# Loading w_in in natural row order, and laying the heads of Y onto the partitions of their features by copies and transfers

## The chip, the cores and the metric

The kernel runs on one core of a Trainium2 chip. A core has five engines with a queue of instructions each: TensorE (PE in the profile; its weight loads are PEld) multiplies matrices from SBUF into PSUM, VectorE (DVE), ScalarE (ACT) and GpSimd (POOL) work elementwise, and SyncE (SP) issues the DMA transfers of this kernel. Every queue is worked off in order. Waits between engines are semaphores, which the tile framework sets from what each instruction reads and writes. The metric is the device time of one execution in microseconds (us), lower is better.

## The reference

Two parts, joined by a transposition. The first is a delta-rule recurrence over 768 positions, for 4 batch elements and 8 heads of dimension 48:

```python
k_n = k / (np.linalg.norm(k, axis=-1, keepdims=True) + 1e-06)
for t in range(S):
    kt, vt, bt = (k_n[:, :, t], v[:, :, t], beta[:, :, t, None])
    y[:, :, t] = np.einsum('bhd,bhde->bhe', q[:, :, t], state)
    v_old = np.einsum('bhde,bhd->bhe', state, kt)
    state = state + bt[:, :, :, None] * np.einsum('bhd,bhe->bhde', kt, vt - v_old)
```

The second takes y as x, 3072 tokens of 384 features (feature = 48 x head + index in the head), through a feed-forward with 2048 hidden units:

```python
x = np.ascontiguousarray(attn_out.transpose(0, 2, 1, 3)).reshape(B * S, H * D)
h = x @ w_in
g = h * (1.0 / (1.0 + np.exp(-h)))
return (g @ w_out).astype(np.float32)
```

q, k, v and beta are float32. w_in (384 x 2048) and w_out (2048 x 384) come as float64: 8 bytes an element, 6.3 MB each.

## The kernel before, in words

**Chunks.** The 768 positions are cut into 6 chunks of 128 (the partitions). A chunk is treated for the 4 batch elements together, in a chain of stages:

- *prepare*: `turn` transposes k and q on TensorE (L376), `score` multiplies them (L399) and masks the products into `ap` on ScalarE and VectorE (L409, L415). `block_out` and `block_in` bring the 32 x 32 diagonal blocks through DRAM into a tile `g` with one block a partition (L443, L451). `block_out` also clears the tile `x` on GpSimd (L438). `scale` and `size` multiply k and v on GpSimd (L352, L360).
- *invert*: the 128 unit triangular blocks (4 batch elements x 8 heads x 4), one a partition, are inverted on VectorE, in 30 steps of two instructions (L477, L481). The results go to DRAM (L492) and come back in two orders into `xe` and `xis` (L502). `invert` is a generator; in chunk 0 the loop that draws it counts the steps as n.
- *solve*: `merge` (L551) joins pairs of blocks, then a pipeline over the batch elements x, with step k from 0 to 6: `inner` and `across` (L583, L591) solve for the new values, `add` (L574) subtracts between the halves on VectorE, `keep` (L601) copies the result z to SBUF on ScalarE, `old` (L614) and `new` (L642, L648) make Y in the PSUM bank `pys[x]`, and `update` (L625, L632) brings the state forward. The norms of the next chunk's keys are drawn in the same loop: `squares` at n = 5 (L306, L309) and `norms` at n = 6 (15 small VectorE instructions from L320 to L338).
- *feed_forward*: `hidden` (L719) multiplies Y, transposed with features on partitions as `xT`, by w_in, two batch elements (256 tokens) at a time. Silu goes through ScalarE (L729). Chunk 0 ends in `project` (L742), the later ones in `combine` (L813), which needs 7 products of half size instead of 8, by adding parts of w_out and of the hidden values (`sum_w`, `sum_g`, L795).

**Order.** The order on every engine is that of the program: `pin` ties each instruction to the one before it on its engine, `in_line` does so for the DMA transfers of SyncE, all in one queue. The feed-forward of one chunk is a generator, `pieces`, and the loops at the end of the program draw from it between the steps of the next chunk's prepare, invert and solve. In the beginning, where there is no feed-forward yet, `busy` issues dummy products (L276): 20 of them follow the 18th step of chunk 0's inversion.

**Weights.** float64 is narrowed on the chip. `narrow` takes three steps over ScalarE (L165, L170), VectorE (L167, L173, L177) and GpSimd (L181) for each of 8 pieces of w_in (256 columns) and 8 of w_out. The raw pieces lie in tiles that are free at that time: the later homes of w_out (`room`), tiles of tag `gT`, sums for `combine` (`sums_of_g`, `sums_of_w`). `fetch_w_in` (L215) and `fetch_w_out` (L245) issue the loads. `queue` holds the pieces to narrow, `fill(n)` issues n steps, `more` fetches a piece of w_out once another is narrowed.

**Where Y's features lie.** A PSUM bank holds Y of one batch element as 4 column blocks of 128 tokens, for the head pairs 0 to 3: even heads on partitions 0 to 47, odd heads on 64 to 111. TensorE wants 3 x 128 features on partitions. So before the change the kernel fills the gaps 48 to 63 and 112 to 127 with thirds of the last pair's heads, and the rows of w_in are loaded in that order:

```python
(at, lambda a, e=e, n=n: (2 * a + e) * D if n == D else (6 + e) * D + a * (W - D), n)
```

That makes 4 transfers a piece: 48 and 16 partitions in each half. In chunks 1 to 5 `new` copies the last pair (L662) and the 48 rows of each half (L665), and 6 transfers carry the thirds (L669). Chunk 0, where the state is zero, gets the thirds from TensorE: `keep` copies a third of the last pair beside each head (L605) and a product more is added for it (L648).

Of the kernel before, what the change touches and what calls it, by code (L numbers as in the profile page):

```python
# [21 lines left out]
def kernel(  # L22
# [120 lines left out]
    for load_one in (load_k, load_q):  # L143
# [4 lines left out]


    ROWS = [  # L150
        (at, lambda a, e=e, n=n: (2 * a + e) * D if n == D else (6 + e) * D + a * (W - D), n)
        for e in range(2)
        for at, n in ((W * e, D), (W * e + D, W - D))
    ]
# [44 lines left out]
    def fetch_w_in(i):  # L199
        if i < 4:  # L200
            raw = room(1 - i // 2, i % 2)
        elif i < NWI - 1:
            raw = mlp.tile([P, SIZE], U32, name="raw", tag="gT", bufs=3)[:]
        else:
            raw = spare
        raw = raw.rearrange("p (a f) -> p a f", a=NKT)
        for at, row, rows in ROWS:
            step = row(1) - row(0)
            src = moe_w_in[row(0) : row(0) + rows, i * WF : (i + 1) * WF].bitcast(U32)
            pitch = src.ap[0][0]  # L210
            src = bass.AP(
                tensor=src.tensor, offset=src.offset,
                ap=[[pitch, rows], [pitch * step, NKT], [1, 2 * WF]],
            )
            in_line(nc.sync.dma_start(out=raw[at : at + rows], in_=src))  # L215
        raws[i] = raw.rearrange("p a (f j) -> p a f j", j=2)
# [7 lines left out]
    sums_of_w = [const.tile([P, NFF // 2, HM], FP32, name=f"sums_of_w{i}") for i in range(3)]  # L224

    def narrow_w_in(i):
        return narrow(w_in[:, :, i * WF : (i + 1) * WF], raws.pop(i))
# [3 lines left out]
    def fetch_w_out(i):  # L231
        if i in (0, 1, 5):
            raw = room(1, min(i, 1))
        elif i in (4, 7):
            raw = sums_of_w[2 if i == 4 else 0][:].rearrange("p f m -> p (f m)").bitcast(U32)
        elif i == 6:
            raw = spare
        else:
            k = int(i == 3)
            if k not in places:  # L240
                places[k] = work.tile([P, SIZE], U32, name="raw_out", tag="ap", bufs=4)
            raw = places[k][:]
        raw = raw.rearrange("p (a f) -> p a f", a=2)
        src = moe_w_out.rearrange("(a p) f -> p a f", p=P)[:, 2 * i : 2 * i + 2, :].bitcast(U32)
        in_line(nc.sync.dma_start(out=raw, in_=src))  # L245
        raws[i] = raw.rearrange("p a (f j) -> p a f j", j=2)

    def narrow_w_out(i):
        at = 2 * i % HFF
        return narrow(w_outs[2 * i // HFF][:, at : at + 2, :], raws.pop(i))  # L250
# [45 lines left out]
    def squares(c):  # L296

        sums[c] = small.tile([P, BH], FP32, name="ss", bufs=1)[:]
        for b in range(B):
            if c == 1:  # L300
                sq = packed(zbufs[b])
            else:
                if b % HB == 0:
                    two = work.tile([P, HB, H, D], FP32, name="sq", tag="xg"[b // HB], bufs=1)
                sq = two[:, b % HB]
            pin(nc.scalar.activation(  # L306
                out=sq, in_=packed(kbufs[(c * B + b) % NK]), func=ACTF.Square
            ))
            pin(nc.vector.tensor_reduce(  # L309
                out=sums[c][:, b * H : (b + 1) * H], in_=sq, axis=AX.X, op=ALU.add  # L310
            ))
# [141 lines left out]
    def invert(c):  # L453
# [41 lines left out]
        if c == 0:  # L495
            xe = sums_of_w[1][:].rearrange("p f m -> p (f m)")[:, 0 : BH * T]
            xes[c] = xe.rearrange("p (n t) -> p n t", n=BH)
        else:
            xes[c] = work.tile([P, BH, T], FP32, name="xe", tag="x", bufs=1)[:]
# [13 lines left out]
    xTs, xes = {}, {}  # L513

    def solve(c, us):
# [6 lines left out]
        pzs, pys, third = {}, {}, {}  # L522
# [5 lines left out]

        if c == 0:
            pin(nc.gpsimd.memset(sums_of_w[0][:], 0.0))  # L530
            thirds = sums_of_w[0][:].rearrange("p f m -> p (f m)").rearrange(
                "p (x k e w) -> p x k e w", x=B, k=NKT, e=2
            )
            third = {x: thirds[:, x] for x in range(B)}
# [65 lines left out]
        def keep(x, rows):  # L600
            pin(nc.scalar.copy(  # L601
                z_of(x)[rows, :, :, 0:D], pzs[x][rows].rearrange("p (a e) d -> p a e d", e=2)
            ))
            if c == 0:
                pin(nc.scalar.copy(  # L605
                    third[x][rows, :, :, D:W],
                    pzs[x][rows, H - 2 : H, :].rearrange("p e (a n) -> p a e n", a=NKT),
                ))
# [28 lines left out]
        def new(x):  # L637
            z, ap = z_of(x), us[x]["ap"]
            for p in range(NP if c > 0 else NKT):
                for e in range(2):  # L640
# [3 lines left out]
                        start=(c == 0), stop=(c > 0), skip_group_check=True,  # L644
                    ))
                for e in range(2 if c == 0 else 0):
                    at = slice(W * e, W * (e + 1)), slice(C * p, C * (p + 1))
                    pin(nc.tensor.matmul(  # L648
                        pys[x][at], lhsT=third[x][:, p, e, :], rhs=ap[:, 2 * NKT + e, 1, :],
                        start=False, stop=True, skip_group_check=True,  # L650
                    ))
            yield
# [8 lines left out]
            last = work.tile([P, C], FP32, name="last")  # L661
            pin(nc.scalar.copy(last[:], pys[x][:, NKT * C : NP * C]))  # L662
            for e, engine in enumerate((nc.scalar.copy, nc.vector.tensor_copy)):
                rows = slice(W * e, W * e + D)
                pin(engine(xT[rows, :, half], of[rows]))  # L665
            n = W - D
            for e in range(2):
                for a in range(NKT):
                    in_line(nc.sync.dma_start(  # L669
                        out=xT[W * e + D : W * (e + 1), a, half],  # L670
                        in_=last[W * e + n * a : W * e + n * (a + 1), :],
                    ))
# [197 lines left out]

    A, CC, M = (psA, "a"), (psC, "c"), (psM, "m")
# [44 lines left out]
    fetch_w_in(2)  # L916
    fetch_w_in(3)
    for i in range(B, 2 * B):
        load_q(i)
    queue, narrowed = deque(), []  # L920

    class Piece:
        def __init__(self, name, steps):
            self.name, self.steps, self.begun, self.done = name, steps, False, 0

        def begin(self):
            if not self.begun:
                next(self.steps)
                self.begun = True
# [18 lines left out]
    queue.extend(Piece(("in", i), narrow_w_in(i)) for i in range(2))  # L948
# [4 lines left out]
    for i in range(B):  # L953
        load_v(i)
    next_us = []
    for n, done in enumerate(invert(0)):
# [3 lines left out]
        if n in (3, 5, 7, 9):  # L960
# [4 lines left out]
    for i in range(4, NWI):  # L965
        fetch_w_in(i)
    fetch_w_out(0)
    squares(1)
    norms(1)
    queue.extend(Piece(("in", i), narrow_w_in(i)) for i in range(2, NWI))  # L970
    queue.append(Piece(("out", 0), narrow_w_out(0)))
# [5 lines left out]
    def more(i, behind=None):  # L977
# [3 lines left out]
        queue.append(Piece(("out", i), narrow_w_out(i)))  # L981

    fill(3)
    for b in range(B):
        size(b)
    more(1, ("in", 1))
    pieces = feed_forward(0)
    for n, _ in enumerate(solve(0, us)):
        fill(2)
        if n == 3:  # L990
            more(2)
            more(3)
            more(4)
# [97 lines left out]
```

## Time and profile before

| | |
|---|---|
| median of 3 runs | 773.38 us (769.96 to 775.83) |
| the profiled execution | 770.21 us |
| its span, first to last instruction | 768.5 us |
| mean granted TensorE clock | 0.977 |
| TensorE busy | 730.4 us (95%), 6806 products |
| its weight loads | 630.0 us (82%) |
| VectorE busy | 411.8 us (54%) |
| ScalarE busy | 233.3 us (30%) |
| GpSimd busy | 83.6 us (11%) |
| DMA | 50.93 MB, mean 66 GB/s |

A busy time is the sum of an engine's instructions. The page's slices give it in tenths for 40 equal stretches of 19.2 us, with the granted clock (PEclk, tenths of full speed), the busy share of the 16 DMA engines and GB/s. The chain that ended last follows the execution back from its last instruction, at each step to what released it; listed in order of time its columns are the start, the duration, the engine, what it did and how many instructions. Timelines list an engine's instructions in the same way. A group of one line (the answers for a line or a tile) gives durations in ns as least, median and greatest, and under it who was waited for: us in total and times. A window's row gives, after its bounds and length, the busy us and instruction counts of PE, PEld, DVE, ACT and POOL, then the granted clock, the DMA share and GB/s.

### The profile page before, as it was taken

How to read it: one execution, taken by the hardware profiler on the slowest of the kernel's cores; microseconds unless marked ns; L12 is line 12 of the kernel's file. 1: busy time of each engine (PE TensorE's matmuls, PEld its weight loads, DVE VectorE, ACT ScalarE, POOL GpSimd, SP SyncE). 2: the span in 40 equal slices, each digit the busy share in tenths (PEclk: the TensorE clock that was granted, in tenths of full speed). 3: DMA queues.
4: the chain of work that ended last, by engine and by line, in shares of the span. 5: the costliest groups of instructions: out<-in, count | busy, mean ns of one | idle time of the engine just before them, and what ended most of it. 6: DMA issues, size and time to landing. Idle time of an engine off the chain costs nothing.

```text
span 768.5 us, 16585 instructions
## 1 busy us (share of the span) xinstructions
PE 730.4 (95%) x6806; PEld 630.0 (82%) x6806; DVE 411.8 (54%) x1050; ACT 233.3 (30%) x512; POOL 83.6 (11%) x95
## 2 busy tenths in 40 slices
PE   7549799899999999999999999999999999999997
PEld 5336587478777999997999997999998999999987
DVE  4886678892336672445672445672445682221212
ACT  4524465311325212315212315212315212312020
POOL 4005246300003000002000002000002000000000
PEclk8859999999999999999999999999999999999999
DMA  9798847212025213034113044113043013010000
GB/s 164 116 167 162 172 146 194 52 66 42 13 54 106 42 48 70 6 77 101 33 49 69 5 77 96 38 49 70 5 77 77 15 49 70 5 30 0 21 1 21
DMA packets 155067, 50.93 MB, mean 66 GB/s; under 512 B 142544, under 2 KB 147536, under 8 KB 154992
## 3 DMA queue, kind: packets, MB, share of 16 engines
q1 hardware_dynamic: 154992, 49.87, 31.1%
q8 instruction: 54, 0.88, 0.5%
q14 instruction: 21, 0.17, 0.1%
HBM read 34.70 MB, written 14.16 MB: 64 GB/s over the span
## 4 chain that ended last, share of the span: by engine, by line
PE 88%; DVE 4%; DMA 3%; SPq 2%; issue 1%; ACT 1%; POOL 1%; ACTq 0%; DVEq 0%
PE phid L719 31%; PE px L813 14%; PE py L813 11%; PE pa L399 6%; PE pz L583 4%; PE pt L376 3%; PE po L742 3%; PE pw L276 3%; PE pyc L642 3%; PE pyc L614 2%; PE ph L567 2%; DMA z<-in_q_dram 2%; PE px L551 2%; PE py L551 2%; PE pu L625 2%; DVE x L481 1%
## 5 line engine op out<-in xcount | busy, mean ns | idle before, releaser
L719 PE MATMUL phid<-xT,w_in 128*128 128x256 f32 x1152 | 260.7, 382 | 2.2 <-ACT gT L729 1.6
L719 PEld LDWEIGHTS phid<-xT,w_in 128*128 128x128 f32 x1152 | 214.8, 190 | 37.2 <-issue 6.3
L729 ACT ACTIVATE gT<-phid 128x512 f32<-128x512 f32 x96 | 57.3, 598 | 189.6 <-PE phid L719 149.2
L415 DVE SCALAR_TENSOR_TENSOR ap<-pa,g,above 128x128 f32<-128x128 f32 x192 | 58.2, 376 | 43.7 <-ACT ap L409 43.7
L481 DVE TENSOR_TENSOR x<-x,rank 128x30 f32<-128x30 f32 (+9 forms) x180 | 59.6, 331 | 7.4 <-ACT x L470 1.1
L477 DVE TENSOR_TENSOR rank<-g,x 128x30 f32<-128x30 f32 (+9 forms) x180 | 59.4, 330 | 5.0
L795 DVE TENSOR_TENSOR sums_of_g<-gT 128x384 f32<-128x384 f32 (+1 forms) x60 | 29.2, 509 | 57.9 <-ACT gT L729 47.3
L813 PE MATMUL py<-w_out,sums_of_g 128*128 128x192 f32 x320 | 56.8, 329 | 0.0
L813 PE MATMUL px<-sums_of_w,sums_of_g 128*128 128x192 f32 x320 | 56.8, 329 | 0.0
L813 PEld LDWEIGHTS px<-sums_of_w,sums_of_g 128*128 128x128 f32 x320 | 52.2, 190 | 1.4 <-issue 1.4
L813 PEld LDWEIGHTS py<-w_out,sums_of_g 128*128 128x128 f32 x320 | 52.2, 190 | 0.4
L409 ACT ACTIVATE ap<-pa,g 128x128 f32<-128x128 f32 x144 | 41.6, 365 | 32.2 <-PE pa L399 32.2
L399 PE MATMUL pa<-kq 48*128 48x256 f32 x384 | 51.0, 401 | 0.2 <-DVE ap L415 0.2
L742 PE MATMUL po<-w_out,gT 128*128 128x384 f32 x128 | 44.7, 495 | 2.9 <-POOL w_out L181 2.9
L399 PEld LDWEIGHTS pa<-kq 48*128 48x128 f32 x384 | 36.9, 192 | 12.1 <-issue 8.1
L583 PEld LDWEIGHTS pz<-vf,xi 64*64 64x64 f32 x768 | 37.3, 138 | 8.5 <-issue 7.3
L583 PE MATMUL pz<-vf,xi 64*64 64x48 f32 x768 | 41.8, 224 | 0.4 <-ACT raw L170 0.3
L601 ACT COPY z<-pz 64x384 f32<-64x384 f32 x48 | 22.7, 474 | 60.8 <-PE pz L583 54.7
L438 POOL MEMSET x<- 128x1024 f32 x6 | 5.7, 950 | 313.5 <-PE pz L583 251.2
L574 DVE TENSOR_TENSOR vf<-vf,ph 128x384 f32<-128x384 f32 x20 | 11.1, 554 | 53.2 <-PE ph L567 53.2
L742 PEld LDWEIGHTS po<-w_out,gT 128*128 128x128 f32 x128 | 23.3, 190 | 18.4 <-POOL w_out L181 4.2
L574 DVE TENSOR_TENSOR vf<-vf,pz 64x384 f32<-64x384 f32 x24 | 13.4, 557 | 42.8 <-PE pz L591 26.0
(132 smaller groups left out, 924.1 us busy)
## 6 DMA issues: line engine op xcount, KB each, us to landing
kb<-in_k_dram SPq DMA_DIRECT2D x24, 192.0 KB, 3.1
z<-in_q_dram SPq DMA_DIRECT2D x24, 192.0 KB, 3.5
vf<-in_v_dram SPq DMA_DIRECT2D x24, 192.0 KB, 3.9
out_dram<-o SPq DMA_DIRECT2D x24, 192.0 KB, 2.0
blocks<-ap SPq DMA_DIRECT2D x96, 32.0 KB, 1.7
g<-blocks SPq DMA_DIRECT2D x24, 128.0 KB, 2.5
up<-x SPq DMA_DIRECT2D x6, 512.0 KB, 2.6
low<-g SPq DMA_DIRECT2D x6, 512.0 KB, 2.9
```

What stands on the lines that cost most here:

```text
L399: u["last"] = pin(nc.tensor.matmul(pa[e][:, pp * 2 * C : (pp + 1) * 2 * C], lhsT=kq[rows, 2 * g + pp, 0, :], rhs=kq[rows, 2 * g + pp, :, : ...
L409: copied = pin(nc.scalar.activation(out=ap[:, h, 0, :], in_=pa[e][:, at : at + C], func=ACTF.Copy, scale=bt[:, h : h + 1],))
L415: masked = pin(nc.vector.scalar_tensor_tensor(out=ap[:, h, j:2, :], in0=pa[e][:, at + j * C : at + 2 * C].rearrange("p (j t) -> p j t", j= ...
L477: pin(nc.vector.tensor_tensor(out=tv, in0=g[:, 0:m, m : m + 1].to_broadcast([P, m, n]), in1=x[:, m : m + 1, m + 1 : T].to_broadcast([P, m, ...
L481: yield pin(nc.vector.tensor_tensor(out=x[:, 0:m, m + 1 : T], in0=x[:, 0:m, m + 1 : T], in1=tv, op=ALU.add))
L551: pin(nc.tensor.matmul(pm[to, at : at + T], lhsT=left, rhs=right, start=True, stop=True))
L583: yield pin(nc.tensor.matmul(pzs[x][rows, h, :], lhsT=xis[x // HB][rows, x % HB * H + h, :], rhs=vs[x][rows, h, :], start=True, stop=True,))
L719: pin(nc.tensor.matmul(ph[:, j * GT : (j + 1) * GT], lhsT=w_in[:, a, (2 * f + j) * P : (2 * f + j + 1) * P], rhs=xTs[c, hf][:, a, :], star ...
L729: pin(nc.scalar.activation(out=gTs[f // FG][:, f % FG, :], in_=ph[:], func=ACTF.Silu, scale=0.5))
L742: pin(nc.tensor.matmul(po[:, 0:DM], lhsT=gTs[f // 2 // FG][:, f // 2 % FG, at : at + C], rhs=w_outs[f // HFF][:, f % HFF, :], start=(f == ...
L795: pin(nc.vector.tensor_tensor(out=sums_of_g[:, k, fs], in0=of[0], in1=of[1], op=op))
L813: pin(nc.tensor.matmul(to, lhsT=at, rhs=quarter(f, *b) if isinstance(b, tuple) else sums_of_w[b][:, f], start=start and f == 0, stop=f == ...
```

## The change

- `ROWS` goes. A piece of w_in is one transfer of 128 partitions, with row 128a + p on partition p: 8 transfers instead of 32.
- The loads of the beginning are issued at other places: pieces 2 and 3 of w_in, then q of chunk 1, v of chunk 0 and piece 4 of w_in, at the second step of chunk 0's inversion; pieces 5 to 7 behind the inversion; then w_out 0, 1 and 4. Chunk 1's transposes come at steps 5, 7, 9, 11 of the inversion instead of 3, 5, 7, 9. All 16 pieces to narrow enter the queue at once, in the same order as before.
- Chunk 0: `keep` also copies heads 1, 2, 5 and 6 into a row of `slab` with gaps, so that any 64 features that lie in two neighbouring heads can be cut out as one window of 64 columns, with zeros where the other head is. `new` adds two products for each group of 64 features: 12 a batch element, as before. The three tiles `sums_of_w` become parts of one tile, in which `slab` and chunk 0's `xe` lie.
- Chunks 1 to 5: the odd heads are copied once to SBUF (`part`, in the slot of `x`), and 5 transfers carry them to their features. The even heads are copied from PSUM to their features by 6 instructions, ScalarE and VectorE in turn.
- `squares` takes both its buffers from the one slot of tag `g`, from chunk 2 on.

```diff
-        for at, row, rows in ROWS:
-            step = row(1) - row(0)
...
-            in_line(nc.sync.dma_start(out=raw[at : at + rows], in_=src))
+        src = moe_w_in.rearrange("(a p) f -> p a f", p=P)[:, :, i * WF : (i + 1) * WF].bitcast(U32)
+        in_line(nc.sync.dma_start(out=raw, in_=src))
...
-                    two = work.tile([P, HB, H, D], FP32, name="sq", tag="xg"[b // HB], bufs=1)
+                    two = work.tile([P, HB, H, D], FP32, name="sq", tag="g" if c > 0 else "xg"[b // HB], bufs=1)
...
+    GAP = W - T
+    SLAB = (D + D + GAP + D) * 2 + D
...
+            pin(nc.gpsimd.memset(sum_room[:, 0 : B * SLAB], 0.0))
+            slab = {x: sum_room[:, x * SLAB : (x + 1) * SLAB] for x in range(B)}
...
+                to = slab[x][rows, D:].rearrange("p (g w) -> p g w", g=2)[:, :, 0 : 2 * (D + GAP)]
                 pin(nc.scalar.copy(
-                    third[x][rows, :, :, D:W],
-                    pzs[x][rows, H - 2 : H, :].rearrange("p e (a n) -> p a e n", a=NKT),
+                    to.rearrange("p g (h w) -> p g h w", h=2)[:, :, :, 0:D],
+                    pzs[x][rows].rearrange("p (g h) d -> p g h d", g=2)[:, :, 1:3, :],
                 ))
...
+            for a in range(NKT if c == 0 else 0):
+                for n in range(2):
+                    for e in range(2):
+                        f = P * a + W * e
+                        h = f // D + n
+                        shift = f - D * h
+                        if h % 4 in (1, 2):
+                            first = D + h // 4 * (3 * D + GAP) + (h % 4 - 1) * (D + GAP)
+                            lhsT = slab[x][:, first + shift : first + shift + W]
+                        else:
+                            lhsT = z[:].rearrange("p a e w -> p (a e w)")[
+                                :, W * h + shift : W * h + shift + W
+                            ]
+                        pin(nc.tensor.matmul(
+                            pys[x][W * e : W * (e + 1), C * a : C * (a + 1)], lhsT=lhsT,
+                            rhs=ap[:, h, 1, :], start=(n == 0), stop=(n == 1),
+                            skip_group_check=True,
+                        ))
...
-            last = work.tile([P, C], FP32, name="last")
-            pin(nc.scalar.copy(last[:], pys[x][:, NKT * C : NP * C]))
-            for e, engine in enumerate((nc.scalar.copy, nc.vector.tensor_copy)):
-                rows = slice(W * e, W * e + D)
-                pin(engine(xT[rows, :, half], of[rows]))
...
+            if x == 0:
+                parts[c] = work.tile([P, 2, NP, C], FP32, name="part", tag="x", bufs=1)
+            part = parts[c][:, x % 2]
+
+            pin(nc.scalar.copy(part[W : W + D], pys[x][W : W + D].rearrange("p (a t) -> p a t", a=NP)))
+            turns = 0
+            for h in chained(range(1, H, 2), range(0, H, 2)):
+                f = D * h
+                while f < D * (h + 1):
+                    n, at = min(D * (h + 1) - f, P - f % P), W * (h % 2) + f - D * h
+                    while h % 2 == 0 and (n > T and at % W or f % P % W and n > T):
+                        n = T
+                    to = xT[f % P : f % P + n, f // P, half]
+                    if h % 2 == 1:
+                        in_line(nc.sync.dma_start(out=to, in_=part[at : at + n, h // 2, :]))
+                    else:
+                        engine = nc.vector.tensor_copy if turns % 2 else nc.scalar.copy
+                        pin(engine(to, pys[x][at : at + n, C * (h // 2) : C * (h // 2 + 1)]))
+                        turns += 1
+                    f += n
...
+    ORDER, TURN, REST = {1: (2, 3, "q", "v", 4)}, (5, 7, 9, 11), (5, 6, 7)
...
-    queue.extend(Piece(("in", i), narrow_w_in(i)) for i in range(2))
+    queue.extend(Piece(kind, i) for kind in ("in", "out") for i in range(NWI))
...
+        for of in ORDER.get(n, ()):
+            if of == "q":
+                for i in range(B, 2 * B):
+                    load_q(i)
+            elif of == "v":
+                for i in range(B):
+                    load_v(i)
+            else:
+                fetch_w_in(of)
+        if n in TURN:
             next_us.append(list(turn(B + len(next_us), M, M))[0])
...
+    for i in (0, 1, 4):
+        more(i, ("in", 1))
```

## The prediction

> **What bounds the kernel now.** I read three things in this order: the page's slices, the chain of work that ended last in order of time, and the timelines of the engines where the chain shows something other than TensorE work.
>
> The slices, 19.2 us each:
>
> ```profile
> PE   7549799899999999999999999999999999999997
> PEclk8859999999999999999999999999999999999999
> DMA  9798847212025213034113044113043013010000
> ```
>
> TensorE is full from the sixth slice on, while DMA is busy at 7 tenths and more only in the first five. In 20 us windows TensorE is busy 20.00 of 20 in every window from 180 to 740 us, and the list of its waits after 170 us has one entry, 1.6 us. So after 170 us nothing but fewer matmuls, or a new stall, moves the end; before it there is idle time to win. The chain of waits there:
>
> ```profile
> 34.40 5.92 DMA w_out<-in_moe_w_in_dram
> 40.34 8.54 DMA z<-in_q_dram
> 48.92 6.20 PE pt L376 x28
> 55.12 12.90 PE pw L276 x40
> 68.03 1.13 PE py L551 x64
> ...
> 80.65 3.02 issue
> ...
> 98.67 2.86 PE phid L719 x12
> ```
>
> The loads of chunk 1's q stand behind two pieces of w_in. TensorE transposes q (28 instructions at half clock), then runs the 20 dummy products (40 instructions) queued behind them, and only then starts the triangular solve (py, 68.03). At 80.65 it stands 3.02 us with nothing to wait for; the DMA answer shows one packet of the instruction queue in that very microsecond, among w_in traffic. The feed-forward starts at 98.67. Between 140 and 170 us come 1.11, 1.80 and 1.64 us more of waits, all at the end of chains that follow TensorE's own progress.
>
> **The change part by part.**
>
> *w_in as one transfer per piece.* The windows of w_in alone and of w_out alone:
>
> ```profile
> 76.00:84.00 8.00, 4.98 (x88) 3.27 (x86) 4.92 (x5) 2.74 (x5) 3.32 (x2) 1.00 1.08 174
> 100.00:104.00 4.00, 4.00 (x58) 3.48 (x58) 1.00 (x4) 1.55 (x4) 1.83 (x1) 1.00 0.93 371
> ```
>
> The last column is GB/s: 174 for w_in in 48- and 16-partition transfers, 371 for w_out in 128-partition ones, both with the DMA engines full. A piece is 768 KB = 786 KB decimal: 4.5 us now. The Trainium skill (SBUF — State Buffer, "Door 1: The DMA port swizzle") says that rate follows how many of 16 ports the partitions of a transfer reach: 48 rows within one half reach 8 (about 218 GB/s), 16 rows 4 (109). Twice 295 KB / 218 + 98 KB / 109 gives 4.5 us, just the measured rate, so the shape is the cause and one transfer should run like w_out: 2.1 us. A rule of the skill speaks against it: DMA: Bandwidth & Descriptors ("Latency and other measured facts") has row pitches that are large powers of two slow, 207 GB/s at 512 KiB. w_in's rows are 16 KiB apart, below its table; by it a piece could take 3.8 us. No row here has this pitch with 128 partitions. I take 2.1 us, since the port sum explains the 174 without the pitch; ends 2.1 and 4.5.
>
> Pieces 2 and 3 stand ahead of q: 2 x (4.5 - 2.1) = 4.8 us earlier q, so transposes from 44.1 instead of 48.9. The dummies need also the 18th step of the inversion on VectorE, done at 47.6: no limit. The solve could start at 68.0 - 4.8 = 63.2. What is late next: the inversion ends at 56.0 whatever DMA does; its results go out and the first come back issued at 60.37 to 61.22, and land 2.5 us later, 63.4 to 63.7. So py starts at about 63.5: **-4.5 us**. Piece 4, now ahead of the inversion's transfers, adds 2.1 us to the queue, which before ran dry at 55.0; 55.0 - 4.8 + 2.1 = 52.3, still before 56.0: free. If pieces kept 4.5 us, it would end at 59.5 and delay the inversion's 1 MB by 3 us, which the dummies (to 68.0) would hide.
>
> SyncE issues 8 transfers where it issued 32, at 0.3 to 1.3 us; it waits for landings, so nothing more is won. The later transposes in the inversion (steps 5 to 11 instead of 3 to 9), the renamed queue of pieces and the order of w_out 0, 1, 4 cost nothing: narrowing stays in the same order on its engines, and TensorE follows neither. w_out 4 arrives earlier, but its reader at 119.0 did not wait. If that cover went, one w_out transfer is 2.1 us.
>
> *The 3.02 us pause.* Solve and pause move ahead by 4.5 us, to about 76. Pieces 5 to 7 (6.3 us from 66.5) have then landed and w_out runs. An instruction packet then meets engines emptied twice as fast. Ends 0 and 3.0; I take **-2.5**, nearer the other instruction packets, at which TensorE did not stop.
>
> *Chunk 0's heads.* 12 products a batch element before and after, same shapes. The added copy doubles (64x96, 232 ns, to 64x192: ScalarE's 128x192 took 331): 8 x 0.1 us, a part of it on the solve's path: **+0.2**. The larger memset (1,600 for 1,536 columns of a 1.37 us one) ends 3 us before its reader.
>
> From 63.5 to 170 us I move everything rigidly, because VectorE, ScalarE, GpSimd and SyncE there follow the solve's steps. That includes SyncE's w_out 5, which waits for the narrowing of piece 1, and chunk 1's v queued behind it. Early sum: -4.5 - 2.5 + 0.2 = **-6.8**.
>
> *Y of chunks 1 to 5 (20 batch elements).* Removed: a 128x128 copy (266 ns), a 48x384 on ScalarE (471) and on VectorE (559), 6 transfers. Added: a 48x512 on ScalarE (128x512 evictions: 586), six copies of 16 to 48 partitions x 128, three on each engine, and 5 transfers. The rows:
>
> ```profile
> L665 ACT COPY xT<-pyc x20: 471/471/472, 209.5 to 680.3; 48x384 f32<-48x384 f32 x20
> L665 DVE COPY xT<-pyc x20: 556/560/561, 210.0 to 680.8; 48x384 f32<-48x384 f32 x20
>   ACT xT L665: 15.6, 13
> ```
>
> The third line is who the second waited for: VectorE's copy waits for ScalarE's, though they read different partitions of the bank. The skill (PSUM — Partial Sum Buffer, "PSUM bank collisions raise a hardware error") says two engines may read one bank at once in different 32-partition groups. By that rule the six copies run as two streams of three, 0.9 us on VectorE; by the row they alternate, six in a row. I go by the row: 0.27 us on ScalarE, about 0.31 on VectorE (559 less 256 elements at the slope of 683 ns for 512), 0.04 for each handover: 2.0 us behind the first copy.
>
> Where does that end? Chunk 2's solve, VectorE, then TensorE:
>
> ```profile
> 322.69 0.56 DVE L665 COPY xT<-pyc 48x384 f32<-48x384 f32 x1
> 323.28 1.36 DVE L795 TENSOR_TENSOR sums_of_g<-gT 128x384 f32<-128x384 f32 x3
> ...
> 328.07 0.56 DVE L574 TENSOR_TENSOR vf<-vf,pz 64x384 f32<-64x384 f32 x1
> ```
>
> ```profile
> 329.24 1.13 PE L583 MATMUL pz<-vf,xi 64*64 64x48 f32 x16
> ```
>
> Behind the copy VectorE has three sums, the 15 small steps of the next norms, and the addition L574 that TensorE's pz at 329.24 reads. Margin: 329.24 - 328.63 = 0.6 us. Two delays come in front. The squares now share one buffer, so ScalarE's third waits for VectorE's second reduction: reductions end 0.55 us later, and so ScalarE's first copy starts at 322.1 and ends at 322.7. The alternation then ends at 324.8 instead of 323.25. L574 comes 1.56 us later: stall 1.0 us. Chunks 3 and 4 show the same margin (444.64 - 444.04, 560.04 - 559.43). Chunk 1 has 1.9 us, chunk 5 no norms. **+3.0 us**; by the streams it would be 3 x 0.3 = 0.9; from below 0, since no copy is dropped from the path. Later in the same solve the second chain holds ScalarE to 332.2; the next evictions have until 335. The bank of one element is needed 5 us later, still free. SyncE's q loads stand behind 5 transfers instead of 6. GpSimd's clearing of x now waits for the last of them (about 342 instead of 320.6), with scaling and v behind it, but v itself arrives only at 345.5.
>
> **Sum.** -6.8 + 3.0 = -3.8. The profiled execution took 770.21 us (768.5 span, 1.7 around it): 766.4. It lies 3.2 below the median of the three runs, 773.38 (769.96 to 775.83); the median should become **769.6**. A measurement of this kernel can hardly tell less than 1% (7.7 us) from no change.
>
> **Rivals.**
> - *No new stall* (0.30): the copies on two engines overlap or find slack. Then 773.4 - 6.8 = 766.6, and as low as 762 if the 4.6 us of waits between 140 and 170 shrink too. For: ScalarE is busy 30%, VectorE 54%. Against: the 0.6 us margin.
> - *Nothing won early* (0.10): the 16 KiB pitch, not the shape, sets 174 GB/s, and the pause stays. 773.4 + 3.0 = 776.4.
> - *Slower* (0.10): the handovers. If one costs 0.3 us and not 0.04, each chain is 1.5 us longer, L574 comes 3.1 us late, and the second chain holds the state updates: about 4.5 us in each of chunks 2 to 4 and 1.5 in chunk 1, +15: 781.6. It decides from about 0.25 us a handover; the VectorE copies that follow ScalarE's by 0.03 speak against it.
>
> **Numbers.** Forecast 769.6 with chance 0.50, own range 766 to 773. The range 763.5 to 777 leaves out about 0.08 below (half the first rival's low end) and 0.10 above (the handovers). Faster by over 1% (under 765.6): over half of the first rival and a tail of the forecast, 0.26. Slower by over 1%: most of the last rival, 0.08. Within: 0.66.
>
> **What would show it.** w_in windows near 370 GB/s; q landed near 44 and py near 63.5; phid first near 92; no pause of 3 us near 76; VectorE copies of xT alternating with ScalarE's; pz waiting about 1 us for L574 in chunks 2 to 4 only. I am wrong if w_in stays under 250 GB/s, if the 20 dummies still end near 68, or if TensorE waits elsewhere after 170 us.

## The result, and the profile after

The kernel after takes 768.02 us (median of 15 runs, 764.12 to 770.34), the kernel before, run beside it, 772.07 us (15 runs, 769.2 to 775.83): ratio 0.9945 (0.9928 to 0.9963), or 4.2 us less (2.8 to 5.6). The forecast was 769.6 us, 3.8 us less. The profiled execution took 767.91 us, span 766.0.

The slices of the kernel after, 19.2 us each, first TensorE, then its granted clock, then DMA:

```profile
PE   7489899899999999999999999999999999999998
PEclk9779799999999999999999999999999999999999
DMA  9797445131154022144012044122043013010000
```

DMA is busy at 9, 7, 9, 7 and 4 tenths in the first five slices, before at 9, 7, 9, 8 and 8: the load of the weights is over sooner. TensorE looks much as before. Its clock differs, in the first three slices (9, 7, 7 for 8, 8, 5) and in the fifth, from 77 to 96 us (7 for 9).

Windows of w_in alone, and of the stretch in which the solve of chunk 0 runs beside pieces 5 to 7 of w_in and pieces of w_out (columns: bounds, length, busy us and counts of PE, PEld, DVE, ACT, POOL, granted clock, DMA share, GB/s):

```profile
12.00:16.00 4.00, 4.00 (x34) 3.17 (x31) 3.00 (x11) 2.99 (x11) 3.01 (x4) 1.00 1.02 363
70.00:80.00 10.00, 8.15 (x161) 5.80 (x163) 9.72 (x11) 5.45 (x10) 5.40 (x3) 0.92 1.03 382
```

w_in now runs at 363 GB/s, as w_out does. The second row shows what is new: VectorE is busy 9.72 of 10 us there. The chain of waits after, in order of time:

```profile
64.84 1.36 PE py L540 x64
...
77.41 0.68 issue
78.09 0.57 DVE vf L563
78.70 0.34 PE pz L572 x2
...
85.69 1.02 PE pu L615 x16
86.71 2.30 PE pyc L650 x24
...
93.43 2.86 PE phid L730 x12
```

The first py group starts at 60.96 (67.96 before), but the feed-forward only at 93.43 (98.67 before): 7.0 us won have become 5.2. The 3.02 us pause is gone. In its place stand waits for VectorE's addition vf at 78.09, and between 80 and 88 us the products run at half clock: a pyc group of 24 takes 2.30 us here and 1.35 at full clock.

After 170 us, TensorE's list of waits has one entry, a new one (that of before, phid waiting 1.6 us for gT, is still there but now ends at 164.8):

```profile
PE pz L572 <- DVE vf L563: 2.9, 3, 1.0
```

Three waits, 2.9 us in all, the longest 1.0. Chunk 2's are in VectorE's timeline and in TensorE's:

```profile
317.93 0.28 DVE L681 COPY xT<-pyc 32x128 f32<-32x128 f32 x1
318.53 0.28 DVE L681 COPY xT<-pyc 48x128 f32<-48x128 f32 x1 [0.32 <-ACT xT L681]
319.14 0.28 DVE L681 COPY xT<-pyc 16x128 f32<-16x128 f32 x1 [0.32 <-ACT xT L681]
319.45 1.36 DVE L806 TENSOR_TENSOR sums_of_g<-gT 128x384 f32<-128x384 f32 x3
...
324.25 0.56 DVE L563 TENSOR_TENSOR vf<-vf,pz 64x384 f32<-64x384 f32 x1
```

```profile
324.87 1.13 PE L572 MATMUL pz<-vf,xi 64*64 64x48 f32 x16 [0.95 <-DVE vf L563]
```

The copies go in turn: VectorE's stand 0.61 us apart, 0.28 of work and 0.32 waiting for ScalarE. Everything behind them is late, and TensorE waits 0.95 us for the addition.

### The profile page after: what moved, and what is told of

Same layout as the page of the kernel before. It is cut to its first block, busy times and chain, and to the rows that moved or that the text cites. A ratio compares the mean times of both kernels' runs of the same rounds, so it can differ in the third digit from the quotient of the medians.

```text
span 766.0 us, 16569 instructions
## 1 busy us (share of the span) xinstructions
PE 730.7 (95%) x6806; PEld 631.0 (82%) x6806; DVE 420.2 (55%) x1090; ACT 247.2 (32%) x552; POOL 84.4 (11%) x95
## 4 chain that ended last, share of the span: by engine, by line
PE 81%; DVE 10%; DMA 3%; ACT 2%; issue 2%; SPq 1%; POOL 1%; ACTq 0%; DVEq 0%
PE phid L730 31%; PE px L824 13%; PE py L824 11%; PE pa L387 5%; PE pz L572 4%; PE po L753 3%; DVE x L469 3%; DVE rank L465 3%; PE ph L556 2%; PE pt L364 2%; PE pyc L632 2%; PE py L540 2%; PE px L540 2%; PE pyc L604 1%; PE pu L615 1%
## 5 line engine op out<-in xcount | busy, mean ns | idle before, releaser
L563 DVE TENSOR_TENSOR vf<-vf,ph 128x384 f32<-128x384 f32 x20 | 11.1, 554 | 53.1 <-PE ph L556 53.1
L563 DVE TENSOR_TENSOR vf<-vf,pz 64x384 f32<-64x384 f32 x24 | 13.4, 557 | 42.1 <-PE pz L580 26.1
```

## The experiments

Each kernel was timed beside runs of the kernel before, so all are given as ratios to it. One sum holds through all the traces and makes them easy to read. Take the span, less the start of phid (the first product of the feed-forward), less TensorE's waits after 200 us. The clocks are those that TensorE was granted in two windows, 12 to 16 us and 76 to 92 us; all else is in us:

| kernel | clock 12-16 | py starts | clock 76-92 | phid starts | waits after 200 | span | rest |
|---|---|---|---|---|---|---|---|
| before | 0.50 | 67.96 | 0.89 | 98.67 | 0 | 768.5 | 669.8 |
| before, once more | 1.00 | 65.28 | 0.79 | 97.12 | 0 | 766.7 | 669.6 |
| before with new Y | 0.50 | 67.14 | 0.89 | 96.79 | 2.9 | 769.4 | 669.7 |
| before, q first | 0.50 | 62.25 | 0.50 | 102.07 | 0 | 771.6 | 669.5 |
| after, four transfers a piece | 0.59 | 67.95 | 1.00 | 95.66 | 2.8 | 768.1 | 669.6 |
| after | 1.00 | 60.96 | 0.68 | 93.43 | 2.9 | 766.0 | 669.7 |
| after, once more | 0.50 | 62.31 | 0.68 | 95.51 | 2.8 | 768.1 | 669.8 |
| after, copies on ScalarE | 0.50 | 63.05 | 0.79 | 94.75 | 0 | 764.4 | 669.7 |
| after, squares apart | 1.00 | 60.40 | 1.00 | 90.03 | 1.6 | 761.3 | 669.7 |
| after, old Y | 1.00 | 60.36 | 0.89 | 90.90 | 0 | 760.5 | 669.6 |
| after, less narrowing | 0.50 | 61.96 | 0.89 | 90.84 | 2.9 | 763.6 | 669.9 |
| after, narrowing later | 1.00 | 60.51 | 0.89 | 89.13 | 2.8 | 768.2 | 676.3 |
| the same, copies on ScalarE | 0.50 | 62.44 | 1.00 | 89.25 | 0 | 765.2 | 676.0 |

In eleven of thirteen the rest is 669.5 to 669.9 us (of the kernel with both edits to copies and squares, the time alone is used). So the change acts in two places alone: it moves the start of phid, and it adds the waits after 200 us. The two others are explained below.

One thing runs beside both. The mean granted clock of each timed run is on record, and among the runs of one kernel the span falls by about 0.5 us for each 0.001 of it. All kernels with the loads of after have more of it, medians of 0.980 to 0.982, where before and the kernels with its loads have 0.976 to 0.978. Taken at one clock by that slope, which is an estimate, old Y lies 4.5 us below before (3.5 to 5.6) where its ratio gives 7.0, and four transfers 0.3 us above it (0.4 below to 1.0 above) where its ratio gives 2.2 below. Whether the moved loads raise the clock, because TensorE stands less, isn't shown. By the sum above, a typical one of the runs of before beside these two (span 769.6 us) begins phid near 99.9 us. Both kept executions of before began earlier, so what makes phid that late may stand in neither trace.

**Four transfers a piece.** After, with w_in's pieces loaded in the old four partition ranges, but natural rows and the new order:

```diff
-        in_line(nc.sync.dma_start(out=raw, in_=src))
+        for at, n in ((0, D), (D, W - D), (W, D), (W + D, W - D)):
+            in_line(nc.sync.dma_start(out=raw[at : at + n], in_=src[at : at + n]))
```

> The changed kernel, but each piece of w_in in four transfers of 48, 16, 48 and 16 partitions (the rows stay in natural order). Theory (the number of partitions of a transfer sets its rate): windows of w_in alone fall from about 360 to about 174 GB/s, chunk 1's q lands about 5 us later than in the changed kernel, the solve of chunk 0 starts near 66 to 68 us, a pause of some 3 us without a named wait comes back at its end; the time rises by 5 us or more, to about 773, above the kernel before. Rival (row pitch or packet size, not the shape, or only clock luck): the windows stay above 300 GB/s and the time stays at 768.

Measured: ratio 0.9971 (0.9956 to 0.9986). In a window of that kernel in which pieces of w_in stream:

```profile
80.00:84.00 4.00, 3.43 (x110) 2.63 (x106) 3.64 (x4) 2.53 (x6) 1.72 (x1) 1.00 1.08 176
```

176 GB/s again, with natural row order, q at 49.51 us and py at 67.95, as before the change. The numbers of partitions of a transfer set the rate. But the kernel is still 2.2 us faster than before although it carries the 2.8 us of new waits, and there is no pause near 80 us. So about 5 us of the early gain come without any earlier py, the forecast of this run (773 us, above before) failed, and the rate is not the whole of it. By the estimate above about 2.5 of the 5 come with a higher clock. What differs from before in this stretch is above all the order: piece 4 of w_in is issued ahead of the inversion's results, at 53.55, where before it followed them at 66.57.

**q first.** The other way round: before, with only the order of q and pieces 2 and 3 exchanged.

```diff
-    fetch_w_in(2)
-    fetch_w_in(3)
     for i in range(B, 2 * B):
         load_q(i)
+    fetch_w_in(2)
+    fetch_w_in(3)
```

> Before, with only the order of loads changed: chunk 1's q ahead of w_in pieces 2 and 3, w_in still in four transfers a piece at 174 GB/s. If q's landing alone held the early part (the order does it): q lands near 41, py starts at 61 to 63.5, no pause of 3 us at px, phid first at 94 to 96, time 2 to 4 below before, ratio 0.995 to 0.997. Rival (the rate does it): q lands near 41 and py starts earlier too, but pieces 2 to 4 land as late as before or later, VectorE's narrowing and the solve behind it wait for them, phid stays near 98, ratio 0.999 to 1.001.

Measured: ratio 1.0010 (0.9986 to 1.0033); py at 62.25, phid at 102.07. The rival came true in the time: 5.7 us won at py, nothing at the end. TensorE stands 5.39 us with no named reason; its timeline at the end of that pause, then ScalarE's around it:

```profile
78.32 1.91 PE L583 MATMUL pz<-vf,xi 64*64 64x48 f32 x16 [5.39 <-issue]
```

```profile
68.81 1.02 ACT L170 ACTIVATE w_out<-w_out,plus 128x768 int32<-128x768 uint32 x1
76.73 0.89 ACT L165 ACTIVATE w_in<-raw 128x768 f32<-128x768 f32 x1 [6.89 <-DMA raw<-in_moe_w_in_dram]
77.65 0.57 ACT L556 COPY xi<-px 32x512 f32<-32x512 f32 x1
```

The copy of xi, which pz reads, ends at 78.22; pz starts at 78.32. The px that it copies had been ready since 71.4. But in ScalarE's queue a narrowing step of w_in piece 4 stands ahead of it, which waits 6.89 us for the piece to land. This is a second gate of the early solve, behind the first one (q and the dummies): the narrowing of pieces that land late holds up, on the same engine, the copies that the solve needs. Then the clock is down too: 0.50 from 76 to 92 us.

**Before, once more, and after, once more.** The same programs, for their traces.

> The kernel before, once more, for its trace alone. Theory (the 3.02 us pause inside px belongs to this program's place in w_in's traffic): it stands again between 78 and 84 us, about 3 us long, and phid starts at 98 to 99. Rival (the pause is an accident of one execution): no pause over 1 us without a named wait, phid at 95 to 97.

> The kernel after, once more, for its trace alone. Theory (VectorE, full with narrowing, and TensorE at half clock around 80 us, both belong to this program): pz waits 1 to 1.7 us for the addition to vf near 79 us, phid at 92.5 to 94. Rival (the half clock comes and goes between executions): phid anywhere from 90 to 94, the lower the higher the granted clock between 80 and 92 us. The three waits of pz after 200 us are 2.9 us in sum in both.

Measured: no pause of 3 us in the second execution of before, and phid at 97.12, as the rival has it. It shows the second gate instead, in ScalarE's timeline:

```profile
74.22 0.89 ACT L165 ACTIVATE w_in<-raw 128x768 f32<-128x768 f32 x1 [2.82 <-DMA raw<-in_moe_w_in_dram]
75.14 0.57 ACT L556 COPY xi<-px 32x512 f32<-32x512 f32 x1
```

pz then starts at 75.81, after a wait of 1.32 us. (The profile names GpSimd's w_in as what it waited for; that ended at 74.82, and the copy of xi, which pz reads, at 75.71.) Before with the new Y, the next run, has the gate too: ScalarE waits 3.38 us for piece 4, and TensorE stands 1.88 us. Over the early stretch ScalarE waits for pieces of w_in 1.5 us in the first execution of before and 6.2 in this one; in the first, TensorE stood 3.02 us by itself instead. In the traces of after ScalarE has no such wait. The second execution of after has the wait for vf (1.3 us) and phid at 95.51, which neither theory named: the clock was half at 12 to 16 us and 0.68 at 76 to 92. One program's phid thus moves by 2 us from one execution to the next, and a difference between two single traces means little below that.

**The new Y alone.** Before, with the new eviction of chunks 1 to 5 and the shared squares' buffer (the two hunks of the diff in `squares` and at the end of `new`, nothing else). w_in keeps its old row order, so the features of Y in chunks 1 to 5 don't stand in w_in's order there.

> Before, with the new eviction of Y in chunks 1 to 5 alone (shared squares' buffer, copies on both engines, five transfers); w_in and chunk 0 stay as they were, so the features of Y of chunks 1 to 5 do not stand in w_in's order. My theory: the steady stall is all that this part does: pz waits for VectorE's addition about 1.0 us in chunks 2, 3 and 4, 2.9 us in all, and the time is 2.9 above before, ratio 1.004. Rival (the stall only shows when the early part has moved things): no such wait, ratio 1.000 within 0.001.

Measured: ratio 1.0023 (1.0004 to 1.0042), 1.8 us more (0.3 to 3.2). In the trace:

```profile
PE pz L583 <- DVE vf L574: 2.9, 3, 1.0
```

The three waits come from this part by itself, whatever goes on early.

**The early part alone.** The reverse: after, with the old eviction of chunks 1 to 5 and two squares' buffers. The features of Y in chunks 1 to 5 stand in the old order while w_in has the new one.

```diff
...
-            part = parts[c][:, x % 2]
...
+            last = work.tile([P, C], FP32, name="last")
+            pin(nc.scalar.copy(last[:], pys[x][:, NKT * C : NP * C]))
...
```

> The early part of the change alone: w_in in one transfer a piece, new order of loads, chunk 0 as changed, but chunks 1 to 5 make Y as before (two copies, six transfers of thirds, squares in two slots). The features of chunks 1 to 5 then lie in another order than the rows of w_in, so the output is not the reference's, while the work is the same. Theory: no waits of TensorE after 170 us, 2.9 us less than the changed kernel: about 765. Rival (the later part costs nothing, the waits are made up elsewhere): 768.

Measured: ratio 0.9909 (0.9885 to 0.9933), 7.0 us less (5.2 to 8.9); no waits after 200 us. The early part is worth what the forecast took for it, 6.8.

**Copies on ScalarE.** After, with all six copies of the even heads on one engine:

```diff
-                        engine = nc.vector.tensor_copy if turns % 2 else nc.scalar.copy
+                        engine = nc.scalar.copy
```

> The changed kernel, but all six copies of even heads on ScalarE. Theory (the alternation of the two engines on one bank delays VectorE's addition that pz reads): the three waits of pz for VectorE in chunks 2 to 4 (2.9 us in sum) vanish, the span falls by about 2.9 us, the time from 768.0 to about 765. The six copies follow one another by about 0.16 us. Rival (the shared buffer of the squares or the longer ScalarE work is the cause): the waits stay near 1 us each, or ScalarE becomes late and TensorE waits for it; the time stays at 768 or rises.

Measured: ratio 0.9905 (0.9883 to 0.9927), 763.66 us. The waits after 200 us are gone. ScalarE's timeline in chunk 2:

```profile
318.13 0.58 ACT L668 COPY part<-pyc 48x512 f32<-48x512 f32 x1
318.73 1.59 ACT L681 COPY xT<-pyc 48x128 f32<-48x128 f32 x6
```

Six copies take 1.59 us in a row, where in turn with VectorE they took 2.13 (ScalarE's first starts at 317.29, VectorE's last ends at 319.42). VectorE has nothing to do with them, and its sums follow its state additions at once. The work that was to be shared is better left on one engine.

**Squares apart.** After, with two buffers for the squares:

```diff
-                    two = work.tile([P, HB, H, D], FP32, name="sq", tag="g" if c > 0 else "xg"[b // HB], bufs=1)
+                    two = work.tile([P, HB, H, D], FP32, name="sq", tag="xg"[b // HB], bufs=1)
```

> The changed kernel, but the two buffers of the squares lie in the slots of x and g, as before. The prediction gave 0.55 of the 1.56 us of delay to the shared buffer: each of the three waits of pz should fall from about 0.97 to about 0.4 us, the time by 1.6 us to about 766.4. Rival (alternation alone): the waits stay at 0.97 us.

Measured: ratio 0.9946 (0.9926 to 0.9966), and in the trace:

```profile
PE pz L572 <- DVE vf L563: 1.6, 3, 0.6
```

Of about 1.0 us a chunk the shared buffer makes 0.4, the copies in turn the rest. 1.3 us is too little for the time itself to show.

**Both.** After, with the two edits above together.

> After, with all six copies of the even heads on ScalarE and the squares in two buffers as before. Theory (what counts is only when VectorE reaches the addition to vf, and ScalarE's copies alone already take that wait away): as with ScalarE's copies alone, 763 to 764.5, ratio 0.990. Rival (the shared squares' buffer costs something besides): another 1 to 2 us less, ratio 0.988.

Measured: ratio 0.9914 (0.9883 to 0.9945): as with the copies alone. With those on ScalarE there is no wait left for the second buffer to shorten.

**Less narrowing.** After, without VectorE's three steps of narrowing for pieces 2, 3 and 4 of w_in; those columns are then not the weights.

```diff
+        if short:
+            yield
+            yield pin(nc.scalar.activation(
...
+            return
```

> After, with the three VectorE steps of narrowing left out for w_in pieces 2, 3 and 4 (their columns of w_in are then not the weights). Theory (in chunk 0's solve VectorE, full with narrowing, gives back what the earlier py won): VectorE is under 3 of 4 us busy between 64 and 80 us, TensorE has no wait for the addition to vf there, phid starts at 89 to 90.5, time about 3 below after: 765, ratio to before 0.990 to 0.992. Rival (TensorE at half clock and the DMA give it back, not VectorE): phid stays at 92 to 94, ratio 0.994 to 0.996.

Measured: ratio 0.9922 (0.9901 to 0.9943), 765.35 us. The stretch from 64 to 76 us in before, in after and in this kernel:

```profile
64.00:76.00 12.00, 12.00 (x218) 7.77 (x217) 7.07 (x8) 4.28 (x6) 8.81 (x8) 1.00 0.96 160
64.00:76.00 12.00, 11.51 (x257) 8.12 (x256) 11.73 (x11) 6.24 (x10) 9.50 (x8) 1.00 0.90 279
64.00:76.00 12.00, 11.52 (x230) 7.57 (x228) 2.95 (x4) 6.54 (x10) 11.31 (x9) 1.00 0.87 267
```

VectorE is busy 2.95 of 12 us here, against 11.73 in after; TensorE has no wait for vf there, and phid starts at 90.84. From py to phid it takes 28.9 us, in after with the old Y at the same clock (0.89) 30.5. So VectorE holds the solve up by about 1.7 us. The two kernels with narrowing later, below, agree: 28.6 us at clock 0.89 and 26.8 at 1.00. In the time it isn't clear of noise (0.9922 to after's 0.9945). The clock acts beside it: with VectorE full, py to phid takes 29.6 us at clock 1.00 (76 to 92 us), 30.5 at 0.89, 31.7 at 0.79, and 32.5 and 33.2 at 0.68. These are single traces. Each theory had a part; neither had all.

**Narrowing later.** After, with one step of narrowing for two in the first five steps of the solve, and w_out 5 fetched behind it. The second kernel has the copies on ScalarE as well.

```diff
-        fill(2)
+        fill(1 if n < 5 else 2)
...
-        if n == 8:
-            more(5, ("out", 1))
...
+    more(5, ("out", 1))
     more(6, ("in", 7))
```

> After, with one step of narrowing in place of two in each of the first five steps of chunk 0's solve, and w_out piece 5 fetched after the solve; nothing is left out. Theory (narrowing on VectorE holds the earlier solve): no wait for the addition to vf before 100 us, phid at 90 to 91, and the steps put off cost nothing: time 2 to 3 below after, 765 to 766, ratio to before 0.991. Rival (the narrowing put off is then late for the projection of w_out): phid at 90 to 91 but 1 to 3 us of new waits of po or phid between 98 and 170 us, time as after, ratio 0.9945.

> The same, with all six copies of the even heads on ScalarE too. The two gains add if both theories hold (narrowing put off: 2 to 3 early; no stall of pz in chunks 2, 3 and 4: 2.9): 761 to 763, ratio 0.987. Rival (the early gain is given back at po): as with ScalarE's copies alone, 763.7, ratio 0.9905.

Measured: ratios 1.0006 (0.9985 to 1.0027) and 0.9963 (0.9946 to 0.9981). phid starts at 89.13 and 89.25, the earliest of all, and both kernels lose 6.3 to 6.6 us behind it. The rival was right in kind and too small in size. ScalarE and TensorE in the first:

```profile
106.43 0.92 ACT L158 ACTIVATE w_out<-raw_out 128x768 f32<-128x768 f32 x1
107.24 1.65 ACT L397 ACTIVATE ap<-pa,g 128x128 f32<-128x128 f32 x6
```

```profile
110.54 3.21 PE L387 MATMUL pa<-kq 48*128 48x256 f32 x14 [1.43 <-DVE ap L403]
113.68 6.45 PE L730 MATMUL phid<-xT,w_in 128*128 128x256 f32 x18
```

The postponed steps fall into chunk 1's prepare, where ScalarE and VectorE make `ap`. ScalarE is busy 8.0 of 8 us from 104 to 112 us. Chunk 1's inversion ends at 166.45 instead of 164.28, though phid began 4.3 us earlier: 6.5 us late, which is the loss. The clock drops as well, and 18 phid products take 6.45 us where at full clock they took about 4.1.

## Why the prediction was right, and where its steps were not

**The rate of w_in: right.** 363 GB/s for the 371 expected. Four transfers a piece bring 176 back with the same rows. The rule of slow row pitches in the Trainium skill (DMA: Bandwidth & Descriptors, "Latency and other measured facts"), which the prediction weighed and set aside, has no bearing here: w_in's rows 16 KiB apart run as fast as w_out. Nor did the 3.8 us a piece follow from it: its 207 GB/s at 512 KiB stand beside 214 that it calls the full rate of those copies.

**py 4.5 us earlier: right, once clocks are compared.** The two profiled executions give 7.0. But they differ in TensorE's clock at 12 to 16 us. With half clock, py starts at 67.96 and 67.14 before, and at 62.31, 63.05, 62.44 and 61.96 in kernels with the loads of after: a mean of 67.55 less one of 62.44 is 5.1. With full clock it is 65.28 and a mean of 60.6 over four: 4.7. As the time of py the step holds. At the end it is worth less: after is only 2.0 us (0.2 to 3.8) faster than four transfers a piece, whose py starts where it did before. The inversion's end, "56.0 whatever DMA does", lies at 54.17 in the profiled after, by that same clock: it is 55.56 in a kernel with the loads of after and half clock (the one with less narrowing).

**"The 3.02 us pause ... -2.5": the wrong cause, and too small.** I took it for an instruction packet held up by w_in's traffic. It belongs to the one execution shown, and what made it there stays open: it stands neither in the second execution of before nor in before with the new Y, and with four transfers a piece w_in's traffic is there and the pause is not. What holds the solve back in that place in the three other traces with before's loads is the second gate, by 1.3, 1.9 and, with q first, 5.4 us. The packet theory would have gained nothing from moving piece 4; I costed that move at nothing ("free"), looking only at the DMA queue and not at what on ScalarE waits for the piece. Four transfers a piece, which has that move and no earlier py, gains 5 us where this step had 2.5 (0.9971, with 2.8 us of waits on board), and without the move q first loses 5.4 of its 5.7 us. That the order of piece 4, and not another of the moves in that order, does it was not tried alone. The waits of ScalarE are the evidence; they account for some 1.3 to 1.9 us of the 5, and the higher clock may account for much of the rest.

**"From 63.5 to 170 us I move everything rigidly": wrong before phid, right behind it.** From phid to the end all is rigid to 0.2 us. Between py and phid it isn't. VectorE, in 64 to 76 us busy 7.07 of 12 us before and 11.73 after, turns to the narrowing only behind the inversion, which did not move by 4.5 us; it gives back about 1.7. The clock gives back 0 to 3.6 more, from one execution to the next. Which of the 7 timed microseconds belongs to which step can't be read more finely than that: single traces of one program stand 2 us apart at phid.

**Chunk 0's heads, +0.2:** too small to be seen; TensorE's wait for the added copy is 1.3 us after, 1.2 before.

**The steady stall, +3.0: right in place, size and parts.** 2.9 us, in chunks 2, 3 and 4, at pz behind L574 (L563 now); 0.4 a chunk from the shared buffer (0.55 forecast), the rest from the copies in turn. They stand 0.61 us apart for two; the forecast had 0.27 + 0.31 + 2 x 0.04 = 0.66. The releasers of these waits are semaphore events, that is, waits in the program, so what the skill says of two engines reading one PSUM bank was not put to the test. Nor did that rule offer the prediction's two streams: the six copies all read partitions 0 to 47, so most neighbours share a 32-partition group. Whether the program makes them wait for the bank that they read or for the tile xT that they write isn't shown. The rival by which a handover costs 0.3 us is excluded: 0.61 less 0.26 and 0.28 leaves 0.03 each.

**The sum.** Early -7.0 (5.2 to 8.9), steady +2.9, together -4.1; forecast -6.8 + 3.0 = -3.8; measured -4.2. Both large terms are confirmed by kernels that hold one alone, the steady one less closely in the time (+1.8, 0.3 to 3.2) than in the trace (+2.9). Inside the early term the shares were wrong: -4.5 for py and -2.5 for the pause were forecast, about -2 for the earlier py and -5 for the rest were measured, a part of the 5 with a higher clock, which the prediction did not count. The two errors cancel, so that the early sum came out so near is luck.

## What to carry to other kernels

When a load is moved, look not only for who reads it but for what stands in the reader's queue behind it: a narrowing step that waits on ScalarE stops the solve's copies, and the profile shows it on TensorE as a pause without a name. Work shared between two engines on one PSUM bank took longer here than on one of them, and it put VectorE late for its next duty: the version with all copies on ScalarE, 763.66 us, is the fastest that leaves nothing out (ratio to before 0.9905, of after 0.9945). And a step that is put off to a later stage is only free if that stage has room on the same engines.

## What the runs showed of the hardware

VectorE's narrowing steps stretch while GpSimd works. The same step of one form, 128 x 768, in VectorE's timeline of after, with GpSimd's at the same time:

```profile
62.68 1.95 DVE L166 TENSOR_SCALAR w_in<-w_in 128x768 uint32<-128x768 uint32 x1
68.65 1.58 DVE L166 TENSOR_SCALAR w_in<-w_in 128x768 uint32<-128x768 uint32 x1
75.05 0.69 DVE L166 TENSOR_SCALAR w_in<-w_in 128x768 uint32<-128x768 uint32 x1
78.68 0.69 DVE L166 TENSOR_SCALAR w_in<-w_in 128x768 uint32<-128x768 uint32 x1
```

```profile
62.18 1.90 POOL L174 TENSOR_TENSOR w_in<-w_in,w_out 128x768 int32<-128x768 int32 x1 [33.55 <-issue]
64.05 4.26 POOL L348 TENSOR_TENSOR vf<-vf,n 128x384 f32<-128x384 f32 x4
68.25 1.43 POOL L522 MEMSET sums_of_w<- 128x1600 f32 x1
69.64 2.02 POOL L174 TENSOR_TENSOR w_in<-w_in,w_out 128x768 int32<-128x768 int32 x1
```

1.58 and 1.95 us beside GpSimd, 0.69 at 75.05, where GpSimd is idle. At 78.68 GpSimd's next addition (76.87, 1.91 us) is all but over. The Trainium skill (SBUF — State Buffer, "SBUF: two separate sides") has VectorE and GpSimd share a pair of ports, which one instruction locks to its end while the other's stands. The rows agree: 0.69 us from the end of GpSimd's instruction (64.08 and 69.68) would be 64.77 and 70.37, and the two long steps end within 0.14 us of that, at 64.63 and 70.23. In after more of the narrowing falls beside GpSimd: L170's three steps on w_out's room took 1.48 us in the mean there and 0.96 before, a part of why VectorE is full. The prediction did not count it.

And TensorE's clock at the start, half or full from 12 to 16 us, changes between executions of the same program (0.50 and 1.00 for before, 1.00 and 0.50 for after) and moves the first solve by 1.4 to 2.7 us. Near 80 us it falls to half in four of five executions with after's early part (after twice, copies on ScalarE, old Y), not in the fifth (squares apart, 1.00 from 76 to 92 us). The skill (TensorE: Matmul & The Clock Gate, "HAM oscillation — how this bites in real kernels") puts such a fall after idle gaps of some 3.4 us. Here no single wait is longer than 1.7 us; what comes before the fall is a stretch in which TensorE is busy for about half the time (1.85 of 3.5 us from 75 to 78.5 us in after, the clock still at 0.98). Half busy alone is not enough: squares apart is busy 1.78 of 3.5 us from 78 to 81.5 us, and its clock stays at 1.00. The measurement decides: several short waits close together can go with such a fall too.
